# Attention and two feed-forward layers on one core: sign masks, score scale and diagonals placed anew

## The chip, the cores and the metric

The kernel runs on one core of a Trainium2 chip. The metric is device time in microseconds (us) of one execution, lower is better; the time of a kernel is the median of several runs. The five engines of the core run their own instruction queues in order: PE (TensorE: matrix products), DVE (VectorE), ACT (ScalarE), POOL (GpSimd) and SP (SyncE, which issues the DMA transfers).

## The reference, cut to what matters

```python
q, k, v: (4, 12, 448, 64)          # batch, heads, sequence, head size; float32
q_n, k_n = rmsnorm(q, g_q), rmsnorm(k, g_k)
attn = softmax(q_n @ k_n.T / sqrt(64))          # row maximum subtracted
x = (attn @ v) -> (1792, 768)
h = x @ w_in                       # (768, 2048)
x = (h * sigmoid(h)) @ w_out       # (2048, 768)
g = x @ w_gate                     # (768, 1536)
out = (silu(g) * (x @ w_val)) @ w_out2          # w_out2 (1536, 768)
```

The weights arrive as float64 and the result is float32.

## The kernel before, in words

Products are made in float16 pairs: a matrix is split in a high half and a low half (the rest), and three products of halves stand for one. The four batches are four blocks. A block has six pairs of heads. Block 0 is special: its first four pairs (`n < N0`) make their scores in float32 with one product, all others with float16 halves; and block 0's probabilities are turned by TensorE, those of the later blocks by DMA transposes. While block 0's attention runs, the chunks of `w_in` are prepared; while its first layer (`ffn1_h`, L1011) runs, those of `w_out`; the later blocks' attention overlaps with both layers of the block before (L1011 and `ffn1_o`, L1051); the gate, value and second output weights are prepared while the last block's layers run. From some 790 us on only the last layers run (L1206, L1250 to L1252).

*Scores* (`softmax_pair`): a score product (L701 in float32, L706 in float16) goes to PSUM, VectorE takes the negative row maximum (L715), a small operation scales it (L718 on ScalarE, L719 on VectorE, L720 on GpSimd), and ScalarE makes the exponential and its sum (L723), with a scale `eS`. In the later blocks high (L739 to L741) and low halves (L744 and L745 on GpSimd, L747 on VectorE) of the probabilities follow, a DMA transpose, and the product with V (L816).

*Weights* (`bring`, `convert`): a chunk of 128x768 float64 numbers lands in a staging tile as pairs of 32-bit words. A scaled copy of the high words, y, is made (L873 ACT, L874 DVE, L875 POOL). Then the sign must be put where it belongs, in one of two ways. With `sign` A or P the low word is shifted (L885) and ScalarE (L887) or GpSimd (L888) writes a float16 number with the sign into its upper half. With `sign` D VectorE masks the sign out of the high word (L879) and shifts some bits of the low word beside it (L880), and no other engine is needed. L890 merges, ScalarE squares and sums (L892), small operations make a scale (L450, L456, L457). Where the low half is made by TensorE (E in the tables, `pe_lo`), a diagonal of the scale is made first (`diag`, L905 on GpSimd, two buffers), the high half is written (L832 to L834), and two matrix products in two halves of 384 columns (L676 in float32, L677) give the low half, which ScalarE copies out (L679). In 14 chunks of `w_out` the low half is made so. Chunks 12 and 14 hold y in XT, chunks 13 and 15 in a raw tile of ATT, so the fourteenth waits for the twelfth.

After the last chunk the scales of all chunks are compared (L445, L971), a product (L441) and L442 spread the maximum, and G is multiplied by the result (L1041 to L1043) before the next layer's first product (L1051).

*The order.* Every operation is recorded with its possible engines, a cost in ns and a due time, and a planner (`Plan.emit`) plays the program through with these costs, giving each operation to an engine and each engine a fixed order. The tables in TUNE hold due times (`FINE`, `OFF`, `WIN`, `WOUT` and others), the allowed engines (letters A, D, P, E) and `WIS`, `WOS`, `GVS`, `O2S`, the sign's engine for each chunk of the five weight matrices. So a change of a cost or a due time moves instructions on every engine.

Of the kernel before, what the change touches and what calls it, by code (L numbers as in the profile page):

```python
# [21 lines left out]
    RIPE_SHORT=1505.0,
# [1 line left out]
    OFF={('load_v', 3): 422.1, ('pv', 3): 8.5, ('qk', 1): -85.8, ('load_qk', 0): -35.2, ('qk', 4): -10.1, ('v_scale', 1): -174.8, ('pv', 1): -9.5, ('soft', 0): -14.2, ('v', 0): -74.0, ('o', 1): 127.6, ('load_v', 0): 121.2, ('qk', 3): -4.5, ('load_v', 4): -203.1, ('h', 2): 116.5, ('v_scale', 2): 58.8, ('v_scale', 3): 122.8, 'w_out': 58.2, 'w_in': 30.8, ('qk', 0): 111.3, ('o', 0): 94.3, ('v', 1): 16.5, ('pv', 0): -6.2, ('h', 1): 362.6, ('v_scale', 0): 43.5, 'h0': -41.4, ('v', 3): 6.8, ('soft', 3): 8.0, ('v', 4): -72.8, 'gv': 130.5, 'x2': 181.6, ('load_qk', 3): 17.7, ('load_qk', 2): 93.7, 'o3': 150.3, 'w2': -104.8, ('v', 2): -25.3, ('load_qk', 4): -5.2, ('load_v', 1): -22.2, ('qk', 2): -34.1, 'f2': -90.5, ('pv', 2): 40.8, ('soft', 2): 61.8, ('pv', 4): 42.7, ('o', 2): 101.1, ('v_scale', 4): -228.9, ('load_v', 2): -52.2, ('load_qk', 1): 19.1, ('soft', 1): 11.3, ('h', 3): -109.0, ('soft', 4): 32.6},
# [6 lines left out]
    BI={'act': -64.7, 'dve': 190.7, 'pool': 150.6},
    T_ATT=109.3,
    STEP0=3.2,
    STEP=21.0,
    WIN=83.7,
    WOUT=99.3,
# [9 lines left out]
    GK=('D', 'P', 'DP'),
    QL=('D', 'D', 'P'),
    VH=('P', 'ADP', 'A'),
    VL=('DP', 'D', 'D'),
    XL=('D', 'D', 'D'),  # L50
# [14 lines left out]
    GVL=('DP', 'DP', 'DP', 'DP', 'DP', 'DP', 'DP', 'DP', 'DP', 'DP', 'D', 'DP', 'D', 'DP', 'DP', 'DP', 'DP', 'DP', 'DP', 'DP', 'P', 'DP', 'D', 'DP'),  # L65
    O2Y=('ADP', 'AP', 'AD', 'D', 'A', 'ADP', 'A', 'AD', 'AD', 'AD', 'AD', 'A'),
    O2S=('D', 'A', 'AP', 'P', 'D', 'D', 'D', 'D', 'D', 'D', 'D', 'P'),
    O2H=('A', 'A', 'DP', 'A', 'A', 'A', 'A', 'A', 'AD', 'A', 'AP', 'A'),
    O2L=('DP',) * 12,
    GH=('AP', 'AD', 'A', 'A'),  # L70
# [1317 lines left out]
```

## Time and profile before

| | |
|---|---|
| median of 3 runs | 1258.47 us (1258.27 to 1259.04) |
| the profiled execution, its own time | 1259.7 us |
| its span, first to last instruction | 1257.9 us |
| TensorE busy | 1178.2 us (94%) |
| VectorE, ScalarE, GpSimd busy | 687.2 us, 669.4 us, 492.0 us |
| mean granted TensorE clock | 0.98 of full speed |

Busy time is summed per engine; the wait of an engine is the idle time just ahead of an instruction, with the engine that ended it. A granted clock of 1 in a stretch means TensorE at 2.4 GHz all through; at the lower of its two levels it runs at 1.2 GHz. The matrix products are pipelined, so neighbouring rows of the timeline overlap by a little.

### The profile page before, as it was taken

The page shows a single profiled execution, that of the slowest core. Times are in us where ns is not written, and L with a number is a line of the kernel's source. Part 1 is how long each engine was busy: PE and PEld are TensorE (multiplying, and loading weights), DVE is VectorE, ACT ScalarE, POOL GpSimd, SP SyncE. Part 2 cuts the span into 40 slices and gives each one's busy share as a digit, 9 for nine tenths or more (in the row PEclk, how much of TensorE's full clock was granted, in tenths as well). Part 3 has the DMA queues.
Part 4 walks back from the last instruction along what each step waited for, and adds up shares of the span by engine and source line. Part 5 has one row for each costly group of instructions (what it writes and reads, how often), then busy time and mean ns, then how long its engine had stood idle before and what let it go on. Part 6 is the DMA issues. An engine that isn't in the chain of part 4 may idle for free.

```text
span 1257.9 us, 17505 instructions
## 1 busy us (share of the span) xinstructions
PE 1178.2 (94%) x6612; PEld 599.2 (48%) x6612; DVE 687.2 (55%) x1181; ACT 669.4 (53%) x1219; POOL 492.0 (39%) x474
## 2 busy tenths in 40 slices
PE   5989987799679999999999999999999999999998
PEld 3334443344334444444445454445544555446685
DVE  4788876688756575565459887873111301112121
ACT  4989967677669865898536435652111301112131
POOL 5565456454658897677721624120000100000000
PEclk9999999799889999999999999999999999999999
DMA  7565634479877688567774455502000101000101
GB/s 193 167 155 144 220 131 145 103 174 199 184 149 144 125 191 176 110 126 149 145 238 138 146 173 180 187 1 63 26 14 1 34 26 26 1 1 22 39 1 26
DMA packets 218581, 140.61 MB, mean 112 GB/s; under 512 B 156032, under 2 KB 210816, under 8 KB 218496
## 3 DMA queue, kind: packets, MB, share of 16 engines
q1 hardware_dynamic: 218496, 139.49, 44.3%
q8 instruction: 52, 0.85, 0.3%
q14 instruction: 33, 0.27, 0.1%
HBM read 85.79 MB, written 11.01 MB: 77 GB/s over the span
## 4 chain that ended last, share of the span: by engine, by line
PE 46%; DVE 5%; DMA 2%; POOL 1%; ACT 1%; issue 1%; POOLq 0%; ACTq 0%
PE ps L1206 25%; PE ps L1051 6%; PE ps L1250 4%; PE ps L1252 4%; PE ps L1251 4%; DMA ATT<-in_moe_w_val_dram 1%; DVE W L842 1%; PE ps L816 1%; PE ps L1011 1%; PE ps L706 1%; DVE ATT L890 1%; DVE G L1030 1%; DVE ATT L880 1%; DVE ATT L879 1%; DMA ATT<-ATT 1%
## 5 line engine op out<-in xcount | busy, mean ns | idle before, releaser
L1206 PE MATMUL ps<-XT,W 128*128 128x512 f16 (+1 forms) x1440 | 294.0, 352 | 3.8 <-ACT ER L1211 1.9
L1051 PE MATMUL ps<-G,W 128*128 128x448 f16 x1152 | 240.7, 355 | 4.0 <-DVE G L1041 4.0
L1011 PE MATMUL ps<-XT,W 128*128 128x448 f16 x1152 | 234.9, 353 | 8.2 <-ACT FT L1017 1.7
L1206 PEld LDWEIGHTS <-W 128*128 128x128 f16 x1440 | 141.0, 98 | 131.0 <-issue 5.1
L1011 PEld LDWEIGHTS <-W 128*128 128x128 f16 x1152 | 110.7, 99 | 120.5 <-issue 26.0
L1051 PEld LDWEIGHTS <-W 128*128 128x128 f16 x1152 | 107.9, 98 | 122.3 <-issue 28.9
L1216 ACT ACTIVATE G<-ER 128x512 f16<-128x512 f32 (+1 forms) x48 | 27.6, 575 | 167.3 <-DVE ER L1213 162.2
L1213 DVE SCALAR_TENSOR_TENSOR ER<-ER,ST,ps 128x512 f32<-128x512 f32 (+1 forms) x48 | 32.6, 680 | 151.5 <-PE ps L1206 151.4
L723 ACT ACTIVATE ER<-ps,ST 128x448 f32<-128x448 f32 x144 | 103.1, 719 | 12.1 <-POOL ATT L745 8.8
L1218 POOL TENSOR_SCALAR G<-ER 128x512 f16<-128x512 f32 x20 | 12.6, 629 | 245.5 <-DVE ER L1217 241.2
L715 DVE TENSOR_REDUCE ST<-ps 128x2 f32<-128x896 f32 x96 | 92.4, 966 | 27.8 <-PE ps L706 23.4
L1250 PE MATMUL ps<-W,G 128*128 128x384 f16 x308 | 100.4, 326 | 0.0
L1251 PE MATMUL ps<-W,G 128*128 128x384 f16 x308 | 100.4, 326 | 0.0
L1252 PE MATMUL ps<-W,G 128*128 128x384 f16 x308 | 100.4, 326 | 0.0
L1257 DVE SCALAR_TENSOR_TENSOR ATT<-ps,ST,ATT 128x384 f32<-128x384 f32 x28 | 17.3, 618 | 151.0 <-ACT ATT L1255 151.0
L1255 ACT ACTIVATE ATT<-ps,ST 128x384 f32<-128x384 f32 x28 | 16.2, 580 | 136.7 <-PE ps L1252 136.7
L745 POOL TENSOR_TENSOR ATT<-ER,ATT 128x448 f16<-128x448 f32 x77 | 86.0, 1117 | 6.4
L706 PE MATMUL ps<-ATT 128*64 128x448 f16 x560 | 75.3, 371 | 9.1 <-ACT ER L723 4.0
L1030 DVE SCALAR_TENSOR_TENSOR G<-FT,ST,G 128x448 f16<-128x448 f32 x64 | 57.5, 907 | 20.1 <-ACT G L1022 18.2
L744 POOL TENSOR_SCALAR ER<-ER,ST 128x448 f32<-128x448 f32 x77 | 56.7, 736 | 22.8 <-ACT ATT L739 11.8
L1206 PE MATMUL ps<-XT,ATT 128*128 128x512 f16 (+1 forms) x288 | 60.4, 352 | 0.0
L739 ACT ACTIVATE ATT<-ER,ST 128x448 f16<-128x448 f32 x71 | 45.5, 660 | 20.0 <-DVE ST L731 11.7
(221 smaller groups left out, 1889.4 us busy)
## 6 DMA issues: line engine op xcount, KB each, us to landing
ATT<-in_moe_w_out_dram SPq DMA_DIRECT2D x24, 768.0 KB, 4.3
W<-in_moe_w_in_dram SPq DMA_DIRECT2D x16, 768.0 KB, 6.1
ATT<-in_moe_w_gate_dram SPq DMA_DIRECT2D x12, 768.0 KB, 4.7
ATT<-in_moe_w_val_dram SPq DMA_DIRECT2D x12, 768.0 KB, 5.9
ATT<-in_q_dram SPq DMA_DIRECT2D x24, 224.0 KB, 3.1
ATT<-in_k_dram SPq DMA_DIRECT2D x24, 224.0 KB, 3.6
ATT<-in_v_dram SPq DMA_DIRECT2D x8, 672.0 KB, 7.2
x2d<-FT SPq DMA_DIRECT2D x24, 224.0 KB, 3.5
```

The costliest lines, as they stand in the source:

```text
L706: nc.tensor.matmul(out=sp[64 * h:64 * h + 64, u, 0:S], lhsT=T[:, 0, t, 64 * h:64 * h + 64], rhs=T[:, a, :, 64 * h:64 * h + 64], start=(a = ...
L715: op(DVE, 1.04 * S * nt + 65, lambda sp=sp, nm=nm, nt=nt: nc.vector.tensor_reduce(nm, sp[:, 0:nt, 0:S], AX.X, ALU.max, negate=True), r=sk, ...
L723: op(ACT, 705, lambda e=e, u=u, t=t, sp=sp: nc.scalar.activation(e, sp[:, u, 0:S], AF.Exp, bias=st["nb"][:, t:t + 1], scale=eS, accum_out= ...
L744: nc.gpsimd.tensor_scalar(e, e, r1, 1.0, ALU.mult, ALU.mult)
L745: nc.gpsimd.tensor_tensor(lo, e, hi, ALU.subtract)
L1011: nc.tensor.matmul(out=ps[:, 0:S], lhsT=w[:, a, kk], rhs=xt1((b * HP + kk) % NX, x), start=(kk == 0 and s == 0), stop=(kk == KD - 1 and s ...
L1030: DVE: (t_stt(S), lambda gt=gt, hi=hi, lo=lo, s1=s1: nc.vector.scalar_tensor_tensor(lo, gt, s1, hi, ALU.mult, ALU.subtract), True),
L1051: nc.tensor.matmul(out=ps[:, 0:S], lhsT=w[:, a, P * m:P * m + P], rhs=GV1[:, f, x], start=(f == 0 and s == 0), stop=(f == NF1 - 1 and s == 2))
L1206: nc.tensor.matmul(out=ps[:, 0:n], lhsT=w[:, aa, kk], rhs=xt2(kk, x)[:, 0:n], start=(kk == 0 and s == 0), stop=(kk == KD - 1 and s == 2))
L1250: nc.tensor.matmul(out=ps[:, 0, 0:384], lhsT=hi, rhs=wh, start=(f == 0), stop=(f == NF2 - 1))
L1251: nc.tensor.matmul(out=ps[:, 1, 0:384], lhsT=hi, rhs=wlo, start=(f == 0), stop=False)
L1252: nc.tensor.matmul(out=ps[:, 1, 0:384], lhsT=lo, rhs=wh, start=False, stop=(f == NF2 - 1))
```

## The change

1. For the first four pairs the factor of the keys is `g_q * g_k * 2^-25` and no longer scaled by the power of two that `eS` undoes, so the scores come out at their own scale: the row maximum is used as it is, the small operation (L718 to L720) is left out, and the exponential's scale is 1.
2. The planner's cost of a sign pass on ScalarE goes from about 793 to 1940 and on GpSimd from 880 to 2030, and in the tables the sign of 15 of the 16 chunks of `w_out` is D.
3. A diagonal may be made on VectorE as well.
4. The small scaling on VectorE is marked as one that shares with GpSimd, and the tables of due times and engines are other ones.

In all VectorE gets 11 sign pairs (L879, L880) more and 11 shifts (L885) fewer, GpSimd 9 sign passes and ScalarE 2 fewer; 13 of 15 diagonals are made on VectorE; 14 low halves of probabilities go from GpSimd to VectorE; 18 low halves of the last layers go from GpSimd to ScalarE. The number of TensorE's instructions is the same.

```diff
-    OFF={('load_v', 3): 422.1, ('pv', 3): 8.5, ('qk', 1): -85.8, ...
+    OFF={('load_v', 3): 411.6, ('pv', 3): 3.7, ('qk', 1): -77.7, ...
...
-    WOS=('P', 'P', 'P', 'AP', 'P', 'A', 'AP', 'AP', 'P', 'P', 'P', 'AP', 'AP', 'AP', 'P', 'D'),
+    WOS=('D', 'D', 'D', 'D', 'D', 'D', 'D', 'D', 'P', 'D', 'D', 'D', 'D', 'D', 'D', 'D'),
...
-    small(mult(gc, gc, g_s), ["gs"], ["gc"], 0)
+    small(lambda: nc.vector.tensor_scalar(gc, gc, 2.0 ** -25, None, ALU.mult), [], ["gc"], 0)
...
+            own = n < N0
+            top = nb if own else nm
...
-            add(only(TUNE["NB"][cl], {
...
+            if not own:
+                add(only(TUNE["NB"][cl], {
...
-                    e, sp[:, u, 0:S], AF.Exp, bias=st["nb"][:, t:t + 1], scale=eS, accum_out=st["sm"][:, t:t + 1]),
+                    e, sp[:, u, 0:S], AF.Exp, bias=st["nb"][:, t:t + 1], scale=1.0 if own else eS, accum_out=st["sm"][:, t:t + 1]),
...
-                ACT: (t_act(n) + 60, lambda: nc.scalar.activation(top, wide, AF.Copy, scale=2.0 ** -60)),
-                POOL: (880, lambda: nc.gpsimd.tensor_scalar(top, wide, 2.0 ** -60, 1.0, ALU.mult, ALU.mult))}), r=ykeys, w=skeys, due=need)
+                ACT: (1940, lambda: nc.scalar.activation(top, wide, AF.Copy, scale=2.0 ** -60)),
+                POOL: (2030, lambda: nc.gpsimd.tensor_scalar(top, wide, 2.0 ** -60, 1.0, ALU.mult, ALU.mult))}), r=ykeys, w=skeys, due=need)
...
-        op(POOL, 351, lambda: nc.gpsimd.tensor_scalar(dg, ID, s1, 2.0 ** 14, ALU.mult, ALU.mult), r=["id"] + sk, w=[("dgw", c)], due=due)
+        add({POOL: (351, lambda: nc.gpsimd.tensor_scalar(dg, ID, s1, 2.0 ** 14, ALU.mult, ALU.mult)),
+             DVE: (200, lambda: nc.vector.tensor_scalar(dg, ID, s1, 2.0 ** 14, ALU.mult, ALU.mult), True)}, r=["id"] + sk, w=[("dgw", c)], due=due)
```

How the order moves is shown at three places. The lines of the changed kernel are 3 higher from `softmax_pair` on (2 for L715, 4 from the diagonal on). The first is VectorE in the first pair's softmax, before:

```order
L715 TENSOR_REDUCE ST<-ps 128x2
L719 TENSOR_SCALAR ST<-ST 128x2
L633 TENSOR_REDUCE ST<-SQ 128x14
L715 TENSOR_REDUCE ST<-ps 128x2
L662 COPY ATT<-ps 64x4x64
L666 TENSOR_SCALAR ATT<-ps,ST 128x256
L666 TENSOR_SCALAR ATT<-ps,ST 128x192
L719 TENSOR_SCALAR ST<-ST 128x2
L715 TENSOR_REDUCE ST<-ps 128x2
```

and in the changed kernel:

```order
L717 TENSOR_REDUCE ST<-ps 128x2 x2
L633 TENSOR_REDUCE ST<-SQ 128x14
L666 TENSOR_SCALAR ATT<-ps,ST 128x256
L666 TENSOR_SCALAR ATT<-ps,ST 128x192
L717 TENSOR_REDUCE ST<-ps 128x2
```

The scalings behind the row maxima (L719) and the copy of transposed queries (L662, now on ScalarE) are gone. The second is VectorE at chunk 14 of `w_out`, the second that goes through XT, before:

```order
L874 TENSOR_SCALAR XT<-ATT 128x768
L874 TENSOR_SCALAR ATT<-ATT 128x768
L885 TENSOR_SCALAR ATT<-ATT 128x768
L879 TENSOR_SCALAR ATT<-ATT 128x768
L880 TENSOR_SCALAR ATT<-ATT 128x768
L1030 SCALAR_TENSOR_TENSOR G<-FT,ST,G 128x448
L890 SCALAR_TENSOR_TENSOR XT<-XT,ATT 128x768
L890 SCALAR_TENSOR_TENSOR ATT<-ATT 128x768
```

and in the changed kernel (L877 is the copy, L882 and L883 the sign pair, L893 the merge, L845 a low half):

```order
L893 SCALAR_TENSOR_TENSOR ATT<-ATT 128x768
L450 TENSOR_SCALAR ST<-ST 128x1
L877 TENSOR_SCALAR XT<-ATT 128x768
L456 TENSOR_SCALAR ST<-ST 128x1
L882 TENSOR_SCALAR ATT<-ATT 128x768
L457 RECIPROCAL ST<-ST 128x1
L883 TENSOR_SCALAR ATT<-ATT 128x768
L893 SCALAR_TENSOR_TENSOR XT<-XT,ATT 128x768
L845 SCALAR_TENSOR_TENSOR W<-ATT,ST,W 128x768
```

Chunk 15 is through before chunk 14 starts, and nothing of chunk 14 up to the merge is on another engine. The third is TensorE between chunks 12 and 14, the two that go through XT, before:

```order
L1011 LDWEIGHTS W
L1011 MATMUL ps<-XT,W 128x448
L676 MATMUL ps<-XT,DG 128x384
L677 LDWEIGHTS NI
L677 MATMUL ps<-W,NI 128x384
L676 MATMUL ps<-XT,DG 128x384
L677 LDWEIGHTS NI
L677 MATMUL ps<-W,NI 128x384
L452 MATMUL ps<-ST 128x1
```

and in the changed kernel:

```order
L677 LDWEIGHTS NI
L677 MATMUL ps<-W,NI 128x384
L676 MATMUL ps<-XT,DG 128x384
L677 LDWEIGHTS NI
L677 MATMUL ps<-W,NI 128x384
L676 MATMUL ps<-XT,DG 128x384
L677 LDWEIGHTS NI
L677 MATMUL ps<-W,NI 128x384
L441 MATMUL ps<-ID,ST 128x128
```

Before, six products of the first layer (L1011) stand between the two chunks; in the changed kernel chunk 14 follows chunk 12 directly, and the product that spreads the maximum (L441) stands ahead of the scores of block 1.

## Rows read from the trace of the kernel before

**Rows 1.** Windows: us; busy PE, PEld, DVE, ACT, POOL; PEclk; DMA share, GB/s.

```profile
138.20:197.70 59.50, 53.45 (x252) 27.17 (x250) 45.32 (x93) 46.97 (x76) 33.69 (x26) 0.97 0.48 168
197.70:220.90 23.20, 15.42 (x60) 7.47 (x60) 17.39 (x33) 16.00 (x29) 12.08 (x12) 0.91 0.47 129
220.90:232.90 12.00, 5.74 (x18) 2.94 (x19) 8.81 (x30) 8.28 (x16) 3.27 (x4) 0.64 0.15 35
318.00:360.00 42.00, 27.77 (x157) 12.45 (x156) 31.30 (x52) 24.91 (x51) 21.89 (x18) 0.80 0.94 196
400.00:800.00 400.00, 389.89 (x2226) 187.21 (x2225) 273.44 (x459) 258.42 (x474) 241.45 (x234) 1.00 0.65 160
800.00:1258.00 458.00, 452.62 (x2562) 250.45 (x2559) 117.08 (x181) 108.52 (x183) 26.05 (x34) 1.00 0.09 26
```

**Rows 2.** TensorE's waits from 120 to 235 us: in total, times, longest.

```profile
PE ps L676 <- POOL DG L905: 12.6, 4, 8.1
PE ps L1051 <- DVE G L1041: 4.0, 1, 4.0
```

**Rows 3.** Timeline of DVE, POOL, ACT, PE, last chunks: start, us; [idle before <- releaser].

```profile
197.67 0.67 DVE L874 TENSOR_SCALAR XT<-ATT 128x768 f32<-128x768 f32 x1
...
213.20 1.53 DVE L874 TENSOR_SCALAR XT<-ATT 128x768 f32<-128x768 f32 x1 [2.61 <-PE ps L676]
214.65 0.55 DVE L874 TENSOR_SCALAR ATT<-ATT 128x768 f32<-128x768 f32 x1
...
216.17 2.59 DVE L880 TENSOR_SCALAR ATT<-ATT 128x768 uint16<-128x768 uint16 x1
...
219.12 0.95 DVE L890 SCALAR_TENSOR_TENSOR XT<-XT,ATT 128x768 int32<-128x768 int32 x1
...
215.76 2.12 POOL L888 TENSOR_SCALAR ATT<-ATT 128x768 f16<-128x768 f32 x1 [1.45 <-DVE ATT L885]
221.78 0.73 POOL L905 TENSOR_SCALAR DG<-ID,ST 128x128 f32<-128x128 f32 x1 [3.90 <-DVE ST L457]
...
220.10 0.84 ACT L892 ACTIVATE ATT<-XT 128x768 f32<-128x768 f32 x1 [4.27 <-DVE XT L890]
...
220.95 2.43 ACT L517 ACTIVATE ATT<-ATT 128x2688 f32<-128x2688 f32 x1
...
211.47 0.88 PE L676 MATMUL ps<-XT,DG 128*128 128x384 f32 x2
...
213.16 1.30 PE L1011 MATMUL ps<-XT,W 128*128 128x448 f16 x6
222.56 1.65 PE L676 MATMUL ps<-XT,DG 128*128 128x384 f32 x2 [8.10 <-POOL DG L905]
...
232.93 1.27 PE L1051 MATMUL ps<-G,W 128*128 128x448 f16 x3 [4.04 <-DVE G L1041]
```

**Rows 4.** VectorE's groups from 138.2 to 197.7: busy us, mean ns | idle before <- releasers.

```profile
L890 DVE SCALAR_TENSOR_TENSOR W<-W 128x768 int32<-128x768 int32 x6 | 7.8, 1301 | 7.0 <-POOL W L888 4.5 <-ACT W L887 2.5
L890 DVE SCALAR_TENSOR_TENSOR W<-W,ATT 128x768 int32<-128x768 int32 x7 | 6.6, 948 | 2.6 <-POOL ATT L888 2.6
...
L842 DVE SCALAR_TENSOR_TENSOR W<-W,ST 128x768 f16<-128x768 f32 x4 | 4.3, 1090 | 0.3 <-ACT W L832 0.3
```

**Rows 5.** Timeline of VectorE and ScalarE at the first exponential.

```profile
19.52 1.18 DVE L719 TENSOR_SCALAR ST<-ST 128x2 f32<-128x2 f32 x1
...
20.79 0.72 ACT L723 ACTIVATE ER<-ps,ST 128x448 f32<-128x448 f32 x1 [1.83 <-DVE ST L719]
```

**Rows 6.** Durations: two lines (ns min/median/max) and one group of VectorE.

```profile
L879 DVE TENSOR_SCALAR ATT<-ATT x28: 547/558/2256, 215.6 to 811.3; 128x768 int32<-128x768 int32 x28
...
L880 DVE TENSOR_SCALAR ATT<-ATT x28: 1018/1033/2586, 216.2 to 812.4; 128x768 uint16<-128x768 uint16 x28
...
L490 DVE TENSOR_SCALAR GX<-GX,ST 128x64 f32<-128x64 f32 x1 | 0.3, 254 | 0.0
```

**Rows 7.** TensorE's waits from 318 to 360 us: in total, times, longest.

```profile
PE ps L816 <- DMA ATT<-ATT: 5.9, 2, 3.7
```

More of the change, by code (lines that the diff above doesn't have):

```diff
@@ L21 @@
     RIPE=0.0,
[L22 removed]
+    RIPE_SHORT=1543.0,
     PATIENCE={'silu': 2351.866, 'exp': 6600.368},
[L24 removed]
@@ L29 @@
+    WIY=('A', 'AP', 'DP', 'P', 'ADP', 'D', 'AP', 'AP', 'ADP', 'AP', 'AP', 'AP', 'DP', 'DP', 'ADP', 'AD'),
+    WOY=('D', 'D', 'D', 'DP', 'D', 'D', 'D', 'AP', 'D', 'AD', 'P', 'D', 'DP', 'D', 'D', 'D'),
+    CUT=(0, 1, 2, 6, 10, 13, 16),
+    SLACK=157.0,
     SLACK2=13.0,
     WT={'act': 0.85, 'dve': 0.99, 'pool': 0.5},
[L31 to L36, printed above, removed]
+    BI={'act': -220.7, 'dve': 190.7, 'pool': 227.0},
@@ L37 @@
+    T_ATT=109.9,
+    STEP0=3.4,
+    STEP=21.1,
+    WIN=93.5,
+    WOUT=92.8,
     ATT1=2.8,
-    PHI1=('AD',) * 7,
-    PHI2=('ADP',) * 7,
+    PHI1=('AD', 'AD', 'AD', 'A', 'A', 'AD', 'AD'),
+    PHI2=('ADP', 'ADP', 'ADP', 'AD', 'ADP', 'AD', 'ADP'),
     PTE=('D', 'A', 'A', 'A', 'A', 'AD', 'AD'),
@@ L42 @@
     PLO1=('DP', 'D', 'DP', 'DP', 'DP', 'DP', 'D'),
-    PLO2=('P', 'P', 'P', 'DP', 'P', 'P', 'P'),
-    RK=('DP', 'P', 'P'),
+    PLO2=('P', 'P', 'P', 'DP', 'P', 'DP', 'P'),
+    RK=('P', 'P', 'P'),
     RQ=('D', 'DP', 'DP'),
[L46 to L50, printed above, removed]
+    GK=('DP', 'P', 'DP'),
+    QL=('P', 'D', 'P'),
+    VH=('AD', 'ADP', 'A'),
+    VL=('D', 'D', 'D'),
+    XL=('E', 'D', 'D'),
     WARM=(12, 7, 6),
     N0=4,
-    TQ='AD',
+    TQ='A',
     TK='D',
@@ L65 @@
[L65 to L70, printed above, removed]
+    WOS=('D', 'D', 'D', 'D', 'D', 'D', 'D', 'D', 'P', 'D', 'D', 'D', 'D', 'D', 'D', 'D'),
@@ L71 @@
+    O2Y=('ADP', 'AP', 'AD', 'D', 'A', 'ADP', 'A', 'AD', 'AP', 'AD', 'ADP', 'A'),
+    O2S=('AP', 'D', 'D', 'P', 'D', 'P', 'D', 'A', 'D', 'A', 'D', 'A'),
+    O2H=('AP', 'A', 'AP', 'A', 'AP', 'AP', 'AP', 'AP', 'A', 'AP', 'AP', 'AP'),
+    O2L=('D', 'ADP', 'D', 'A', 'P', 'D', 'D', 'AP', 'D', 'A', 'D', 'D'),
+    GH=('ADP', 'DP', 'AP', 'A'),
     GL=('DP', 'D', 'D', 'DP'),
@@ L714, in softmax_pair @@
             sm, rr = st["sm"][:, t0:t0 + nt], st["rr"][:, t0:t0 + nt]
-            op(DVE, 1.04 * S * nt + 65, lambda sp=sp, nm=nm, nt=nt: nc.vector.tensor_reduce(nm, sp[:, 0:nt, 0:S], AX.X, ALU.max, negate=True),
-               r=sk, w=[("nm", i, g)], due=due)
-            add(only(TUNE["NB"][cl], {
-                ACT: (200, lambda nm=nm, nb=nb: nc.scalar.activation(nb, nm, AF.Copy, scale=eS)),
-                DVE: (130, lambda nm=nm, nb=nb: nc.vector.tensor_scalar(nb, nm, eS, None, ALU.mult)),
-                POOL: (246, lambda nm=nm, nb=nb: nc.gpsimd.tensor_scalar(nb, nm, eS, 1.0, ALU.mult, ALU.mult))}), r=[("nm", i, g), "eS"], w=[("nb", i, g)], due=due)
+            own = n < N0
+            top = nb if own else nm
+            op(DVE, 1.04 * S * nt + 65, lambda sp=sp, top=top, nt=nt: nc.vector.tensor_reduce(top, sp[:, 0:nt, 0:S], AX.X, ALU.max, negate=True),
+               r=sk, w=[("nb" if own else "nm", i, g)], due=due)
+            if not own:
+                add(only(TUNE["NB"][cl], {
+                    ACT: (200, lambda nm=nm, nb=nb: nc.scalar.activation(nb, nm, AF.Copy, scale=eS)),
+                    DVE: (130, lambda nm=nm, nb=nb: nc.vector.tensor_scalar(nb, nm, eS, None, ALU.mult), True),
+                    POOL: (246, lambda nm=nm, nb=nb: nc.gpsimd.tensor_scalar(nb, nm, eS, 1.0, ALU.mult, ALU.mult))}), r=[("nm", i, g), "eS"], w=[("nb", i, g)], due=due)
             for u, t in enumerate(tiles):
                 e, ek = es[t]
-                op(ACT, 705, lambda e=e, u=u, t=t, sp=sp: nc.scalar.activation(
-                    e, sp[:, u, 0:S], AF.Exp, bias=st["nb"][:, t:t + 1], scale=eS, accum_out=st["sm"][:, t:t + 1]),
+                op(ACT, 705, lambda e=e, u=u, t=t, sp=sp, own=own: nc.scalar.activation(
+                    e, sp[:, u, 0:S], AF.Exp, bias=st["nb"][:, t:t + 1], scale=1.0 if own else eS, accum_out=st["sm"][:, t:t + 1]),
                    r=[sk[u], ("nb", i, g)], w=ek + [("sm", i, t)], due=due, table="exp")
```

18 lines of the change are left out of this document (8 added, 10 removed).

## Prediction

> **What bounds the kernel now.** I read busy time and granted clock by stretch first. From 800 us on TensorE is busy 452.6 of 458 us, from 400 to 800 it is busy 389.9 of 400 [rows 1]: whatever the change does to the other engines there, it can return about 10 us at most. The time that can be won lies ahead of 400 us, where an engine that feeds TensorE is late. So I went to TensorE's own waits in the stretch where `w_out` is prepared: 12.6 us in four waits for a diagonal made on GpSimd, 8.1 of them in one, and 4.0 us for the first product of the next layer [rows 2]. The timeline of the last chunks shows the order of events [rows 3]: VectorE starts the first chunk that goes through XT at 197.67, its product runs on TensorE at 211.47, the second XT chunk may overwrite XT only then (213.20), its signs are on GpSimd until 217.9, its diagonal is written at 221.78, TensorE restarts at 222.56 and the next layer's first product starts at 232.93. In the 12 us before that the granted clock is 0.64, part of the stretch at the lower of the two levels (1.2 GHz) [rows 1], and the same product takes 1.65 us instead of 0.88 [rows 3]: TensorE had stood still for 8.1 us.
>
> What keeps the chunks is told by VectorE's groups from 138.2 (its first low half of G) to 197.7: it is busy 45.3 of 59.5 us [rows 1], and of its 14.2 idle us 7.1 (4.5 + 2.6) end with a sign pass on GpSimd [rows 4].
>
> **The change, part by part.** The profiled execution took 1259.7 us (span 1257.9), 1.2 us above the median 1258.47 of the runs shown. Sums are made against the profiled time.
>
> *Scores at their own scale (first four pairs).* The small scaling between the row maximum and the exponential goes. The first one took 1.18 us on VectorE because it stood beside GpSimd's work, and ScalarE sat idle 1.83 us until it was done [rows 5]. Sixteen such operations go, but ScalarE is busy nearly all of the time afterwards, so most of them are covered by other exponentials. Copies of the transposed queries move to ScalarE and cost a little of it back. Bounds 0 and -4 us (1 us in each of the four pairs); taken: **-2 us**, near that one idle time.
>
> *Signs on VectorE, diagonals on VectorE.* I take VectorE from its first low half of G to the first XT chunk. By the program order it issues there 12 more half-word shifts of 1.03 us (the median, [rows 6]) = 12.4; 12 more maskings of 0.56 [rows 6] less 10 word shifts of the same size = 1.1; 10 diagonals; two more low halves of G and some eight other operations, together 3.4. A diagonal of 128x128 float32 on VectorE is not in the trace: the nearest rows are 0.25 us for 128x64 and 0.56 for 128x768 [rows 6], and I take 0.3, near the smaller, so 3.0; at the ends 2.5 and 5.6. Sum +19.9 us of work. What goes: the 7.1 us of waiting for GpSimd's signs, and the stretching of the merges beside GpSimd, 1301 against 948 ns, six times, 2.1 us [rows 4]. Of the other 7.1 us of idle I let 3.5 go, since a queue that holds more work of its own finds the other engines' results ready. The first XT chunk starts 19.9 - 7.1 - 2.1 - 3.5 = **7.2 us later** in the stage.
>
> From there to the next layer the path gets shorter. For the second XT chunk the scaled copy took 1.53, the sign pass on GpSimd 2.12 and the bit shift of its neighbour 2.59 us; from 213.20 to the end of the merge (219.12 + 0.95) 6.9 us went by [rows 3]. The order of the change runs copy, mask, shift and merge on one engine: 0.55 + 0.56 + 1.03 + 0.95 = 3.1, **-3.8 us**. The first XT chunk waited for a sign pass on ScalarE and for a diagonal behind other work of GpSimd: 197.67 to 211.47 is 13.8 us [rows 3]. In the new order VectorE does 4.4 us up to the merge (copy, a neighbour's merge, masking, diagonal and shift, its own merge), ScalarE squares (0.84, [rows 3], and some 0.2 for reading the sum), and VectorE does 2.5 us up to the diagonal (a low half of 1.09, [rows 4], a copy, a masking, the diagonal): 7.9, **-5.9 us**. ScalarE's square over v (2.43 us at 220.95) now stands behind the last weight square instead of ahead of one; I count nothing for it, since the reduction that follows on VectorE waits for it. What takes the cover away: in the new order of TensorE nothing of the first layer is left between the two XT chunks, so it waits out the whole preparation of the second, some 5 us, in place of 1.3 us of work and 8.1 of waiting. The stage's end moves by 7.2 - 3.8 - 5.9 = **-2.5 us**; with the rest of that idle gone as well it is -6.1, with no more gone than GpSimd's 7.1 it is +1.0.
>
> *Block 1.* TensorE waits 5.9 us for two transposes of probabilities (3.7 and 2.2 us) ahead of the fifth and sixth product with V [rows 7], between 318 and 360 us, where VectorE is busy 31.3, ScalarE 24.9 and GpSimd 21.9 of 42 us [rows 1]: no engine is full, the pair's chain is. In the new order sixteen score products stand directly behind the fourth product with V, and directly behind the fifth; before, 21 and 9 products of the layers stood ahead of them, at some 0.2 us each (six took 1.30, [rows 3]) 4.2 and 1.8 us. GpSimd also has fewer low halves to make (14 over the kernel go to VectorE). Bounds 0 and -5.9; taken **-3 us**, since the two leads are 6.0 together and the softmax of a pair still needs three engines.
>
> *The rest.* The gate and value weights get three masks fewer on VectorE and more high halves on ScalarE, both beside TensorE's work, which is 97% busy there [rows 1]: 0, and at most a few microseconds either way if a chunk comes late. Low halves in the last layer move from GpSimd to ScalarE, while TensorE runs without a gap: 0.
>
> Sum: -2 - 2.5 - 3 = -7.5; 1259.7 - 7.5 = 1252.2, and as a median (1.2 lower) **1251 us**.
>
> **The rivals.** *VectorE becomes the bound of the `w_out` stage, and the kernel gets slower.* The stage gives VectorE 19.9 us more work, and in the order printed every step of a chunk but the square now queues on it. If its idle time stays as it is (14.2 us) the first XT chunk starts 17.8 us later, not 7.2, and the stage ends 8.1 us later. The row for it is a shift that took 2.59 us while GpSimd's sign pass ran from 215.76 to 217.88 [rows 3]: it ended 0.9 us after that pass, so it was held. The Trainium skill, SBUF — State Buffer, section Who interferes with whom, says that VectorE and GpSimd share a port pair as an exclusive lock, and that an operation with one input outside the two-port modes does not contend; by the lock every mask that meets GpSimd waits, by the exception the shift would not have, and this row sides with the lock. Priced from the row, each mask that meets GpSimd costs 1.56 us; two or three of 12 would, since GpSimd has 13 operations in that stretch of its order, where it had 38: 4 us. Then -2 + 8.1 + 4 = +10, and with or without block 1's 3 us 1266 to 1269. It decides from the point where the first XT chunk starts more than 9.7 us later in the stage (what the tail gives back), about 11.7 with the start's 2 us. For it: 45.3 + 19.9 is more than 59.5. Against it: half the idle time there is waiting for just the passes that go.
>
> *The diagonals were the whole story.* All 12.6 us of waits for diagonals go, and VectorE's idle time with them; half of the 4.0 ahead of the next layer goes too, since the last scales come sooner; with -2 and -3 elsewhere and some microseconds for the gap between the XT chunks left: about -16, 1242. For it: GpSimd loses 9 sign passes and 13 diagonals in this stage. Against: the same chunks must pass VectorE.
>
> *Nothing arrives.* VectorE's added work eats the stage's gain (+1.0), the start gains 2, and block 1 nothing, because a transpose that starts sooner meets the next pair's loads (the DMA engines are 0.94 busy there, [rows 1]): 1259.7 - 1 - 1.2 = 1257.5. That the change does not do what it says is covered here: if the scheduler left signs on GpSimd, but the printed order has 11 sign pairs more on VectorE in all and 9 passes fewer on GpSimd.
>
> **How the numbers follow.** Forecast (1247 to 1255): 0.42. Diagonals the whole story (1238 to 1247): 0.23. Nothing arrives (1256 to 1261): 0.16. VectorE the bound (1261 to 1269): 0.19. A measurement of this kernel can tell about 0.2%, 2.5 us, from no change; so faster 0.65, same 0.16, slower 0.19. The range 1239 to 1268 leaves out the outer ends of the second and last case, under 0.1.
>
> **What would show it.** Right: TensorE's waits for a diagonal fall from 12.6 us to under 8, the first product of the next layer starts some 4 us sooner (near 228 to 229), its waits for a transposed probability fall to about 3 us, and the idle time from 400 on stays near 10 + 5 us. Wrong: VectorE is busy over nine tenths from 140 to 220 and the second XT chunk's copy starts after 216 (the first rival), masks of over 2 us appear beside GpSimd (its price), or new waits of TensorE show up between 650 and 800 for weights that come late.

## The result and the profile after

The changed kernel takes **1238.18 us** (median of 4 runs, 1235.70 to 1240.69) beside 1258.76 for the kernel before (4 runs): ratio 0.9837, 95% interval 0.9816 to 0.9858, or 20.6 us less. The forecast was 7.5 less, with a range of 1239 to 1268. In two later comparisons the ratio was 0.9815 [0.9792, 0.9839] and 0.9821 [0.9796, 0.9846].

The profiled execution took 1238.76 us, its span 1236.9 (before 1257.9): 21.0 less. TensorE's busy time fell from 1178.2 to 1172.6 for the same number of products: fewer stretches ran at the lower of the two clock levels (mean granted clock 0.985 for 0.98). The other 15.4 us are idle time of TensorE. Working out idle as length less busy, by stretch: 0 to 140 us, 25.6 before and 20.6 after; 140 to 240, 20.1 and 13.0; 240 to 400, 18.5 and 19.2; 400 to 800, 10.1 and 6.2; from 800 on, 5.3 and 5.3.

Four windows of the changed kernel answer to [rows 1] (us; busy PE, PEld, DVE, ACT, POOL; PEclk; DMA share, GB/s): the stage from VectorE's first low half of G to the first XT chunk, its end, block 1's softmax, and 400 to 800 us.

```profile
130.40:192.40 62.00, 58.58 (x280) 29.56 (x278) 59.89 (x124) 50.23 (x89) 12.59 (x10) 1.00 0.49 177
...
206.50:216.90 10.40, 5.67 (x19) 2.86 (x20) 7.37 (x24) 9.33 (x14) 3.10 (x3) 0.67 0.14 44
300.00:342.00 42.00, 26.72 (x168) 13.74 (x165) 27.70 (x52) 24.32 (x52) 23.66 (x18) 0.84 1.02 204
400.00:800.00 400.00, 393.82 (x2238) 190.12 (x2235) 272.75 (x479) 272.94 (x488) 203.05 (x188) 1.00 0.63 162
```

VectorE is now busy 59.9 of 62 us in that stage (before 45.3 of 59.5), GpSimd 12.6 (before 33.7). TensorE's waits from 120 to 235 us, as in [rows 2]:

```profile
PE ps L676 <- POOL DG L908: 6.1, 1, 6.1
PE ps L676 <- ACT W L679: 2.7, 3, 1.4
PE ps L1055 <- DVE G L1045: 2.2, 1, 2.2
```

The timeline of the last chunks, as in [rows 3] (L877 copy, L882 and L883 sign pair, L893 merge, L908 diagonal on GpSimd, L1055 the next layer; VectorE, GpSimd, then TensorE):

```profile
192.42 0.56 DVE L877 TENSOR_SCALAR XT<-ATT 128x768 f32<-128x768 f32 x1
192.90 0.95 DVE L893 SCALAR_TENSOR_TENSOR ATT<-ATT 128x768 int32<-128x768 int32 x1
193.76 0.56 DVE L882 TENSOR_SCALAR ATT<-ATT 128x768 int32<-128x768 int32 x1
...
203.34 0.56 DVE L877 TENSOR_SCALAR XT<-ATT 128x768 f32<-128x768 f32 x1
...
204.53 1.03 DVE L883 TENSOR_SCALAR ATT<-ATT 128x768 uint16<-128x768 uint16 x1
...
205.59 0.96 DVE L893 SCALAR_TENSOR_TENSOR XT<-XT,ATT 128x768 int32<-128x768 int32 x1
...
208.26 0.72 POOL L908 TENSOR_SCALAR DG<-ID,ST 128x128 f32<-128x128 f32 x1 [10.42 <-DVE ST L445]
...
201.02 0.91 PE L676 MATMUL ps<-XT,DG 128*128 128x384 f32 x2 [0.85 <-ACT W L679]
...
209.04 1.65 PE L676 MATMUL ps<-XT,DG 128*128 128x384 f32 x2 [6.13 <-POOL DG L908]
...
216.87 1.47 PE L1055 MATMUL ps<-G,W 128*128 128x448 f16 x4 [2.19 <-DVE G L1045]
```

The next layer's first product starts at 216.87 in place of 232.93: 16.1 of the 21.0 us are won by there, and the same 946 products stand ahead of it in both kernels.

### The profile page after: what moved, and what is told of

Read it like the earlier page. It is cut to its first block, busy times and chain, and to the rows that moved or that the text cites. A ratio compares the mean times of both kernels' runs of the same rounds, so it can differ in the third digit from the quotient of the medians.

```text
span 1236.9 us, 17468 instructions
## 1 busy us (share of the span) xinstructions
PE 1172.6 (95%) x6612; PEld 600.4 (49%) x6612; DVE 678.7 (55%) x1210; ACT 693.5 (56%) x1260; POOL 402.6 (33%) x374
## 4 chain that ended last, share of the span: by engine, by line
PE 47%; DVE 3%; DMA 1%; ACT 1%; issue 1%; POOL 1%; ACTq 0%; POOLq 0%; DVEq 0%
PE ps L1210 25%; PE ps L1055 7%; PE ps L1254 4%; PE ps L1256 4%; PE ps L1255 4%; DVE W L845 1%; DVE G L1034 1%; DVE ATT L893 1%; PE ps L819 1%; PE ps L1015 1%; DMA ATT<-in_moe_w_out_dram 0%; DMA x2d<-FT 0%; DVE ATT L883 0%; PE ps L706 0%; DMA ATT<-in_moe_w_val_dram 0%
## 5 line engine op out<-in xcount | busy, mean ns | idle before, releaser
L1055 PE MATMUL ps<-G,W 128*128 128x448 f16 x1152 | 241.4, 355 | 2.2 <-DVE G L1045 2.2
L1055 PEld LDWEIGHTS <-W 128*128 128x128 f16 x1152 | 108.1, 98 | 120.4 <-issue 26.7
L1015 PEld LDWEIGHTS <-W 128*128 128x128 f16 x1152 | 110.9, 99 | 114.5 <-issue 19.3
L726 ACT ACTIVATE ER<-ps,ST 128x448 f32<-128x448 f32 x144 | 102.3, 713 | 14.6 <-POOL ATT L748 7.5
L717 DVE TENSOR_REDUCE ST<-ps 128x2 f32<-128x896 f32 x96 | 92.1, 966 | 31.8 <-PE ps L706 25.7
L706 PE MATMUL ps<-ATT 128*64 128x448 f16 x560 | 74.1, 362 | 5.5 <-ACT ER L726 3.0
L748 POOL TENSOR_TENSOR ATT<-ER,ATT 128x448 f16<-128x448 f32 x63 | 71.7, 1138 | 5.3
L742 ACT ACTIVATE ATT<-ER,ST 128x448 f16<-128x448 f32 x84 | 53.2, 659 | 10.8 <-DVE ST L734 6.5
L819 PE MATMUL ps<-ATT 128*64 128x448 f16 x396 | 44.6, 377 | 14.3 <-DMA ATT<-ATT 14.2
```

The source lines that it names most:

```text
L706: nc.tensor.matmul(out=sp[64 * h:64 * h + 64, u, 0:S], lhsT=T[:, 0, t, 64 * h:64 * h + 64], rhs=T[:, a, :, 64 * h:64 * h + 64], start=(a = ...
L717: op(DVE, 1.04 * S * nt + 65, lambda sp=sp, top=top, nt=nt: nc.vector.tensor_reduce(top, sp[:, 0:nt, 0:S], AX.X, ALU.max, negate=True), r= ...
L726: op(ACT, 705, lambda e=e, u=u, t=t, sp=sp, own=own: nc.scalar.activation(e, sp[:, u, 0:S], AF.Exp, bias=st["nb"][:, t:t + 1], scale=1.0 i ...
L748: nc.gpsimd.tensor_tensor(lo, e, hi, ALU.subtract)
L819: nc.tensor.matmul(out=PS_X[64 * h:64 * h + 64, 0:S], lhsT=vv[:, h, b, :], rhs=PT[:, :, b, 64 * h:64 * h + 64], start=(s == 0), stop=(s == ...
L1015: nc.tensor.matmul(out=ps[:, 0:S], lhsT=w[:, a, kk], rhs=xt1((b * HP + kk) % NX, x), start=(kk == 0 and s == 0), stop=(kk == KD - 1 and s ...
```

## The experiments

Most kernels below keep **every queue in the order that the planner gave it**: an edit is made where an operation is emitted, not where it is planned, so TensorE's and SyncE's queues are the same row for row, and only the operation in question changes its engine or goes (the order of the changed kernel is the new order, that of the kernel before the old one). That separates the edits from the new order, which the diff alone mixes. Events of the profiled executions (us; "product 1" is the first of the first layer, "product 2" the first of the next, XT the copies of the two chunks through XT):

| kernel | product 1 | XT, XT | product 2 | span | from product 2 to the end |
|---|---|---|---|---|---|
| before | 120.4 | 197.7, 213.2 | 232.9 | 1257.9 | 1025.0 |
| g1: own scale | 114.3 | 192.7, 208.3 | 228.0 | 1252.5 | 1024.5 |
| g2: signs | 121.1 | 195.1, 209.9 | 228.5 | 1251.0 | 1022.5 |
| g3: diagonals | 120.4 | 196.0, 211.0 | 230.8 | 1253.4 | 1022.6 |
| g4: all three | 114.9 | 188.7, 203.6 | 222.7 | 1246.1 | 1023.5 |
| changed kernel | 112.4 | 192.4, 203.3 | 216.9 | 1236.9 | 1020.0 |
| f1: scaling back | 116.2 | 197.3, 208.2 | 221.5 | 1240.2 | 1018.7 |
| f2: diagonals back | 112.5 | 191.9, 203.6 | 217.2 | 1233.6 | 1016.4 |
| f3: signs back | 110.9 | 197.9, 211.6 | 226.1 | 1243.3 | 1017.2 |
| f5: all back | 118.8 | 205.4, 219.8 | 234.1 | 1252.0 | 1018.0 |
| r1: old tables | 111.7 | 199.2, 215.7 | 231.1 | 1251.8 | 1020.7 |

Three profiles of the changed kernel itself differ by 1.3 us in product 2 and 1.9 in the span; less than that between two rows says nothing.

### The edits in the old order (g1 to g4)

```diff
-            op(DVE, ..., nm=nm, nt=nt: nc.vector.tensor_reduce(nm, ...
+            op(DVE, ..., top=nb if n < N0 else nm, nt=nt: nc.vector.tensor_reduce(top, ...
-                DVE: (130, lambda nm=nm, nb=nb: nc.vector.tensor_scalar(nb, nm, eS, ...
+                DVE: (130, lambda nm=nm, nb=nb, own=n < N0: None if own else nc.vector.tensor_scalar(nb, nm, eS, ...
...
-            op(DVE, 470, lambda: nc.vector.tensor_scalar(lw, lw, 29, ...
+            op(DVE, 470, mask if mine else lambda: nc.vector.tensor_scalar(lw, lw, 29, ...
-                POOL: (880, lambda: nc.gpsimd.tensor_scalar(top, wide, ...
+                POOL: (880, slip if mine else lambda: nc.gpsimd.tensor_scalar(top, wide, ...
...
-        op(POOL, 351, lambda: nc.gpsimd.tensor_scalar(dg, ID, ...
+        op(POOL, 351, lambda: nc.vector.tensor_scalar(dg, ID, ...
```

The first part is g1, the second g2 (mask and slip are the two operations of L879 and L880, for `w_out` alone), the third g3; g4 has all.

> The kernel before with every queue in its old order; only the scores of the first four pairs come at their own scale, and the small scalings there (L718 to L720) are left out. Theory A (the edit itself is worth what the first four pairs gained, since the exponential waited for a scaling that stood behind other work in VectorE's queue): the first product of the first layer moves from 120.4 to about 113, the kernel to about 1251 (-8 us). Theory B (the edit is worth the -2 us that I gave it; the rest of the 8 us came from the new order): 1255 to 1258.

Measured: 0.9961 [0.9946, 0.9976], 4.9 us: between the two theories. Product 1 comes 6.1 us sooner by this edit alone, three quarters of the 8.0 that the whole change gains there. What the 6.1 us consist of is read below, in the part on the prediction: 2.2 are waiting, 3.9 a faster TensorE.

> The kernel before with every queue in its old order; only the sign pass of 15 chunks of w_out (GpSimd or ScalarE) is replaced, in its place, by the mask and the half-word shift on VectorE. Theory A (the passes between the engines are what the stage loses): the second XT chunk's preparation shortens by some 3 to 4 us, VectorE's 7.1 us of waiting for signs go, the next layer's first product comes 4 to 6 us sooner than 232.9, the kernel ends near 1253. Theory B (VectorE's queue is full in that order, and the masks only pay in the new one): within 2 us of before, or up to 5 us slower.

Measured: 0.9949 [0.9931, 0.9966], 6.4 us; product 2 is 4.4 us sooner. Theory A. VectorE has 54.6 us of work from 140 to 200, where it had 45.8, and still the first XT chunk starts 2.6 us earlier: its waits for GpSimd's signs (7.1 us) are gone.

> The kernel before with every queue in its old order; only the diagonals are made on VectorE, in their place, instead of GpSimd. Theory A (diagonals were late because they stood behind GpSimd's sign passes): TensorE's 12.6 us of waits for diagonals fall under 5, the next layer's first product comes 6 to 8 us sooner, the kernel ends near 1251. Theory B (the diagonal was late because its scale was): the same waits stay, now for VectorE, at 8 us or more, and the time stays within 2 us of before.

Measured: 0.9967 [0.9955, 0.9980], 4.2 us, between the two theories. The wait behind the second XT chunk stays, now for VectorE; the small ones go:

```profile
PE ps L676 <- DVE DG L905: 9.9, 2, 8.6
```

> The kernel before with every queue in its old order and all three edits at once: scores at their own scale, signs of w_out on VectorE, diagonals on VectorE. If the edits make the gain: near 1240, at most 3 us above the changed kernel's 1238.2. If the new order of the queues makes most of it: above 1248. Rival of the prediction (VectorE becomes the bound): above 1255, with VectorE busy over nine tenths from 140 to 220 us.

Measured: 0.9917 [0.9896, 0.9938], 10.4 us: half of the gain, and less than the 15.5 us that the three edits gave one by one. The order of the old tables holds the rest. In it VectorE copies the second XT chunk at 203.57 and merges it only at 209.06, since chunk 15 goes through the same queue between the two; the diagonal still waits:

```profile
PE ps L676 <- DVE DG L905: 8.5, 3, 7.7
PE ps L1051 <- DVE G L1041: 3.8, 1, 3.8
```

### The edits undone in the new order (f1, f2, f3, f5, f6)

f1 puts a multiplication by 1 behind each row maximum of the first four pairs; f2 and f6 emit the 13 diagonals with `nc.gpsimd`; f3 puts the word shift and the sign pass in the place of the mask and the half-word shift; f5 does all.

> The changed kernel with every queue in its order; only a scaling (by 1) is put back on VectorE directly behind each row maximum of the first four pairs. In the kernel before, taking the scalings out of the old order gave 5 us; there they stood up to three operations behind their maximum. Theory A (what they cost was their place in the queue): directly behind the maximum each costs its own 0.2 to 0.6 us on a VectorE that is 0.75 busy, so the first product of the first layer moves by 1 to 3 us and the kernel ends 1 to 3 us later, 1239 to 1241. Theory B (the hop itself is what costs): some 6 us later, near 1244.

Measured: 0.9875 [0.9839, 0.9911], 5 to 8 us above the changed kernel by the ratios, 3.3 by the spans; product 1 is 3.9 us later. Between the two theories, and more than A: the sixteen operations are 5.7 us of VectorE (12 of 0.42, 4 of 0.15), and product 1 feels 3.9 of that, though nothing stands between the maximum and its scaling. In the old order (g1) it was 6.1; the 2.2 us between are little more than the 1.1 by which product 1 differs between profiles of the changed kernel.

> The changed kernel with every queue in its order; the 13 diagonals made on VectorE are made on GpSimd, in their place. GpSimd is busy only 10 of the 60 us from 140 to 200 in that order. Theory A (a diagonal was late because GpSimd was full): it now costs only its longer duration and the way to another engine, 0 to 3 us, 1238 to 1241. Theory B (VectorE is the right place whatever the load): 6 us or more, above 1244.

> The changed kernel with every queue in its order and the 13 diagonals on GpSimd, as in f2_diagonals_back, now beside the changed kernel. There the next layer's first product came at 217.19, in the changed kernel at 216.87. If diagonals on VectorE are worth nothing in the new order: within 2 us of the changed kernel. If they are a loss there: 3 to 5 us faster than it, as the two separate comparisons with before (0.9797 and 0.9837) have it. If they are a gain: 2 us or more slower.

Measured: 0.9797 [0.9757, 0.9837] in f2, 0.9814 [0.9787, 0.9840] in f6, beside 0.9815 for the changed kernel on the same chip. Nothing: what looked like a gain in f2 was scatter. With one sign pass of `w_out` left on GpSimd, a diagonal is as good there; TensorE then waits 2.9 us for diagonals that it did not wait for, and 1.8 less for ScalarE.

> The changed kernel with every queue in its order; the signs of 14 chunks of w_out are put on GpSimd (one on ScalarE) again, in their place, with the word shift on VectorE. Theory A (the new order leans on signs being on VectorE; a chunk now waits for a pass of about 2 us in the middle of VectorE's queue): each of the chunks that follow each other closely adds 1 to 2 us, the next layer's first product comes 10 to 20 us later than 216.9, the kernel ends between 1248 and 1260. Theory B (the signs' engine matters little and the order makes the gain): within 6 us, the same size as in the old order, 1238 to 1245.

Measured: 0.9885 [0.9851, 0.9920]: 6 to 9 us above the changed kernel by the ratios, at the upper end of theory B. Product 2 comes 9.2 us later, just short of theory A's 10 to 20, twice what the signs were worth in the old order, but the span only 6.4; the difference lies behind product 2, within what the last column scatters. It is not quite a way back: f3 makes 14 signs of `w_out` on GpSimd and one on ScalarE, the kernel before made 10 and 5.

> The changed kernel with every queue in its order and all three edits undone in their place: the scaling behind the maximum, diagonals and signs on GpSimd. The old order with the three edits gave 0.9917 of before, half of the gain. If the two halves simply add (edits 10 us, order 10 us): near 1249. If the new order only works with the edits: at the old time of 1258 or slower, up to 1270.

Measured: 0.9940 [0.9919, 0.9960], nearer to a sum of two halves than to no gain. The new order alone gives about 7 us, and by the table none of it ahead of product 2 (234.1, before 232.9): the first XT chunk comes 7.7 us later and the way from it to product 2 is 6.6 us shorter (28.7 for 35.3). There the order pays only with the edits. What it gives is behind: from product 2 to the end the kernels that keep the new order take 1015 to 1020 us, those that keep the old one 1022 to 1025. No run takes that part of the order apart.

### What makes the order, and what holds the stage's end

> The code of the changed kernel (own scale, the new costs of a sign pass, diagonals on either engine), planned anew with the tables of the kernel before, except that w_out's signs are on VectorE as in the change. Theory A (the planner makes a good order by itself once the costs are right): near the changed kernel, 1238 to 1243. Theory B (the new due times and engines in the tables make the order): what the three edits gave in the old order, 1248 to 1252, or worse.

Measured: 0.9943 [0.9922, 0.9964], theory B. The planner, with the corrected costs and free diagonals but the old due times and engines, reaches product 1 as soon as the changed kernel and then loses all of it in the stage. Its waits for diagonals add up to more than in any other kernel:

```profile
PE ps L676 <- POOL DG L908: 19.5, 5, 7.7
```

All diagonals of `w_out` are on GpSimd there, but GpSimd was not what was late. The first stands at 177.6 us (166.3 in the changed kernel), and in this row of GpSimd's own waits it waits for the scale from VectorE, which is busy 48.6 of 60 us from 140 to 200, in the changed kernel 58.0:

```profile
POOL DG L908 <- DVE ST L457: 30.1, 4, 25.6
```

The tables hold due times and allowed engines; which of the two leaves VectorE idle there no run separates.

The next two move chunk 14 out of XT; the planner orders anew.

```diff
-                y, yk = XT[:, 12 * S:12 * S + 1536].bitcast(F32), [...]
+                y, yk = (ER[:, 2:4]..., [("e", 2), ("e", 3)]) if c == 14 else (XT[...].bitcast(F32), [...])
```

> The changed kernel with chunk 14 of w_out in a part of ER in place of XT, so that it need not wait until TensorE has read chunk 12; the planner then orders anew around it. TensorE's longest wait in the changed kernel (6.1 us, for chunk 14's diagonal) lies there. Theory A (sharing XT holds the end of the stage): that wait falls under 3 us, the next layer's first product comes 3 to 5 us sooner than 216.9, the kernel ends near 1234. Theory B (VectorE, 0.96 busy from 140 to 200, holds it; the shared tile costs nothing): the product comes within 2 us of 216.9 and the kernel within 3 us of 1238.

Measured: 0.9820 [0.9794, 0.9847]. Product 2 at 214.57, 2.3 us sooner, TensorE's longest wait 4.1 in place of 6.1, and no gain in the kernel: TensorE is idle 22.1 us from 300 to 400, 4 more than in the changed kernel. So the shared tile holds at most some 2 us of the end (the planner's order moved too), and block 1 took them back.

> As x1_third_tile, but chunk 14 lies in the first raw tile of ATT, where the next block's first q and k are loaded afterwards. Theory A: as there, less what the later load costs: 1234 to 1238. Theory B: within 3 us of 1238, or slower where the load delays block 1.

Measured: 0.9985 [0.9973, 0.9998]: product 2 at 222.46, and idle 29.4 us from 300 to 400 (100 less 70.65 busy). The planner's new order here is worse in both places; on the shared tile it says nothing.

> The changed kernel with every queue in its order; the two diagonals still made on GpSimd are made on VectorE. The last one took 0.72 us there and starts 0.17 us after its scale; VectorE has a high half of 0.62 us and a small operation ahead of it. Gain of the next layer's first product by 0 to 1 us; the kernel within 2 us of the changed one, 1236 to 1240.

Measured: 0.9792 [0.9774, 0.9810]. The wait for the last diagonal falls from 6.13 to 5.65, as the rows foretold. By the ratios the kernel is 3 to 6 us faster than the changed one; its interval overlaps those of the two later comparisons, but not the first. y1, below, has the same diagonals and stands beside the changed kernel on one chip.

### Block 1's transposes

In block 1 TensorE's waits for transposed probabilities rose (below). SyncE's queue, where each transpose of probabilities stands for 3.6 to 5.0 us, has its rows nearly end to end from 280 to 340. h1 and h2 take three loads per pair out of it.

```diff
-        op(SP, ..., lambda: nc.sync.dma_start(out=dst[0:64], in_=src), ...
+        op(SP, ..., lambda: (nc.gpsimd if b == 1 else nc.sync).dma_start(out=dst[0:64], in_=src), ...
```

> The changed kernel with every queue in its order; only the three loads of v of each pair of block 1 (0.65 us of SyncE's queue each, 1.9 of some 17 us per pair) are issued by GpSimd. In the changed kernel TensorE waits 13.1 us for transposed probabilities between 290 and 345, and SyncE's queue has no gap from 280 to 340. Theory A (SyncE's queue, where every transpose takes 3.6 to 5 us, sets the pace of block 1): a pair passes some 2 us sooner, the waits for transposes fall from 13 to under 8, the kernel gains 2 to 5 us. Theory B (the DMA engines, busy 1.03 in that stretch, set the pace): the waits stay at 11 to 15 us and the time within 2 us of the changed kernel.

> As h1_v_on_gpsimd, but the loads of v of block 1 are issued from ScalarE's queue. Theory A: SyncE's queue is relieved as much, but ScalarE, 0.76 busy in block 1, takes the issues into its own queue, between the exponentials: waits for transposes under 10 us, waits for exponentials up by 1 to 3, the time 0 to 4 us below the changed kernel. Theory B: waits for transposes stay, the time is the same or up to 3 us above.

Measured: 0.9829 [0.9804, 0.9853] and 0.9809 [0.9785, 0.9834], beside 0.9815 for the changed kernel. Theory A falls: TensorE still waits for the transposed probabilities ahead of the same two products, 8.9 us in h1 and 11.5 in h2, part of it now put down to the softmax that feeds them; in h1:

```profile
PE ps L819 <- DMA ATT<-ATT: 6.9, 1, 6.9
PE ps L706 <- ACT ER L726: 4.6, 5, 2.0
PE ps L441 <- DVE ST L1065: 2.6, 1, 2.6
PE ps L819 <- DVE ST L734: 2.0, 1, 2.0
```

> The changed kernel with every queue in its order, all diagonals on VectorE (as in f4_last_diagonals, where the next layer's first product came at 215.70) and the loads of v of block 1 issued from ScalarE's queue (as in h2_v_on_scalar). Alone each was at most 0.3% below the changed kernel, inside what the intervals allow. If both are real: 3 to 5 us below the changed kernel beside it. If they were scatter: within 2 us of it.

Measured: 0.9809 [0.9783, 0.9835], the changed kernel beside it 0.9821: the same within the noise. No version was found that is measurably faster than the changed kernel.

## Why the prediction was wrong, step by step

**The start: -2 forecast, -7.8 found** (VectorE's first low half of G at 130.44 for 138.19; product 1 8.0 sooner). The step that failed is pricing the sixteen operations by "that one idle time" alone: the sum has waits and no term for TensorE's clock, which it puts at nothing without a reason. Four windows from 0 to product 1, in the kernel before, g1, f1 and the changed kernel, columns as in [rows 1]:

```profile
0.00:120.37 120.37, 96.02 (x528) 47.56 (x529) 89.32 (x159) 95.09 (x189) 69.52 (x75) 0.94 0.61 168
0.00:114.30 114.30, 92.13 (x528) 47.05 (x529) 82.65 (x149) 92.32 (x189) 67.52 (x69) 0.97 0.63 172
0.00:116.24 116.24, 94.52 (x526) 48.34 (x527) 84.95 (x163) 92.71 (x189) 65.84 (x65) 0.96 0.62 170
0.00:112.39 112.39, 92.20 (x526) 47.32 (x527) 80.69 (x147) 92.38 (x189) 65.07 (x65) 0.97 0.64 176
```

In g1 the same 528 products take 92.1 us of TensorE's busy time in place of 96.0, at a granted clock of 0.97 for 0.94, and its idle time (length less busy) falls from 24.4 to 22.2. So 3.9 of the 6.1 us are faster products and 2.2 are waiting, the forecast's -2. g2 and g3, which keep the scaling, have 97.1 and 95.8 us busy there; g4, which leaves it out, has 93.1. In the whole change 3.8 of the 8.0 us are busy time and 4.2 waiting, just past my lower bound of -4, so the new order adds 2.0 of waiting; the operations put back (f1) cost 2.3 and 1.5. The waiting went down although ScalarE was not "busy nearly all of the time": 113.5 of the first 140 us before, so 26.5 were open (11.3 of them waits for the first loads), and the chain of a pair (scores in one of two PSUM buffers, maximum, scaling, exponential, next scores in that buffer) passed through every scaling.

**The stage up to the first XT chunk: 7.2 us longer forecast, 2.5 found** (59.5 to 62.0). Two terms were off. The added work was put at 19.9 less 2.1 of stretching, 17.8; VectorE's busy time rose by 14.6. I had added durations of rows, and rows of VectorE overlap: the copy at 192.42 lasts 0.56 and the next operation starts 0.48 later. The 124 rows of the stage add up to 71.2 us for 59.9 of busy time, the 93 of before to 51.9 for 45.3: 19.3 us more of durations, near the forecast, but only 14.6 more of busy time. And the idle time, of which I let 10.6 go, fell by 12.1, from 14.2 to 2.1, nearly all: with most signs on VectorE there is always something to do. g2 shows the same in the old order. TensorE was nearly full in this stage as well, busy 58.6 of 62 us with 28 more products in it than before (53.5 of 59.5), so a longer stage is not a loss: its own idle time there fell from 6.0 to 3.4.

**From there to the next layer: -9.7 forecast, -10.8 found** (35.3 to 24.5). Right, and by its own parts: the second XT chunk from its copy to the end of its merge 3.2 us (6.9 before; -3.7 for -3.8 forecast), the first from its copy to its product 8.6 (13.8; -5.2 for -5.9). The last 1.9 us are the end of the merge to product 2, less 0.6 between the two. The wait of TensorE between the two chunks is 6.1, forecast at some 5. But g4 has the same edits and keeps 34.0 us there, and f5 has the new order without them and needs 28.7: most of this gain comes from the order, where chunk 15 stands ahead of chunk 14, as the second excerpt of the orders showed.

**Block 1: -3 forecast, nothing found.** The waits for transposes were to fall from 5.9 to 3 us; they rose to 12.1 at the same two products ([rows 7]; TensorE's timeline, L819 is the product with V):

```profile
315.01 4.32 PE L819 MATMUL ps<-ATT 128*64 128x448 f16 x22 [5.08 <-DMA ATT<-ATT]
...
333.19 3.92 PE L819 MATMUL ps<-ATT 128*64 128x448 f16 x22 [7.03 <-DMA ATT<-ATT]
```

The products with V of the second to sixth pair stand 17.6 us apart on average before (278.70 to 349.00) and 16.7 after (266.58 to 333.19): a pair's chain takes nearly as long. I had read score products that "stand directly behind the fourth product with V" as a lead of 6 us; but with the layers' products taken from between, TensorE only comes to the wait sooner. These two products start 17.0 and 15.8 us earlier than before, about the 16.1 that were won by product 2. The idle time from 300 to 400 is 17.7 before and 18.1 after. What sets the pace of 16 to 18 us is not SyncE's queue alone (h1, h2); whether it is the softmax's chain or the DMA engines, busy 1.00 of the time from 280 to 340, stays open.

**The rest: 0 forecast, about -4 found.** Idle from 400 to 800 fell from 10.1 to 6.2, within the few microseconds that I allowed and in one direction. It goes with the order, not with the edits (the last column of the table).

In sum: -5.8 (start), -4.7 (stage), -1.1 (tail), and -2.0 behind product 2 (-5.0 found, -3 forecast) make, before rounding, the 13.5 us by which -7.5 missed -21.0. Of these, 5.6 are TensorE's busy time (3.8 ahead of product 1, 1.7 behind product 2), for which the forecast had no term. Of the signs named beforehand, the waits for a diagonal (6.1, under 8) and the idle time from 400 on (11.5 for 10 + 5) came as said; product 2 came 16 us sooner in place of 4, and the waits for transposes rose.

**The rivals.** "The diagonals were the whole story" has the nearest time (1242) for the wrong reason: diagonals gave 4.2 us in the old order (g3) and nothing in the new (f6), and the largest wait for one is still there. "VectorE becomes the bound" named its first sign rightly (busy 0.92 from 140 to 220) but not its second (the second XT copy after 216; it came at 203.3): VectorE was full, with less work than I had added up, and no mask took over 1.9 us. "Nothing arrives" fails by the 20.6 us; only its part on block 1 came true. The price of the second rival exists, but few operations paid it: of the twelve half-word shifts in the stage eleven took 1.0 us, and one took 1.61:

```profile
186.02 1.61 DVE L883 TENSOR_SCALAR ATT<-ATT 128x768 uint16<-128x768 uint16 x1
...
185.81 0.93 POOL L837 TENSOR_SCALAR W<-W,ST 128x768 f16<-128x768 f32 x1 [1.85 <-PE ps L1015]
```

GpSimd's operation began 0.21 us ahead of the shift and ended at 186.74; from there to the shift's end at 187.63 it is 0.89 us, nearly a whole shift. In the kernel before, all five such shifts that began while a GpSimd operation ran ended 0.87 to 0.89 us after it. The Trainium skill, SBUF — State Buffer, section Who interferes with whom, has an exclusive lock for this pair, held for a whole instruction, and exempts VectorE's operations with one input outside the two-port modes. The rows agree with the lock. No run shows in which mode the shift ran, so neither these rows nor the prediction's speak against the exemption. GpSimd had 10 operations in the stage (26 before), so few shifts met one.

## What to carry to other kernels

Where a change takes waits away from TensorE, price its clock too: here leaving out sixteen operations won 2.2 us of waiting and 3.9 of faster products, and only busy and idle time read apart show it. Add up an engine's start-to-start times, not its durations. And where a change brings new tables of due times, try the edits in the old order and the old operations in the new one: here the order alone gave some 7 us, the edits alone some 10 and both 21, and the forecast had costed the edits only.

## What the runs showed of the hardware

A sign pass (768 float32 to float16 written at every fourth place) took 1.89 to 2.49 us on GpSimd in the 13 that f3 puts back there (1.90 where no VectorE row stood beside it) and 1.91 to 2.03 on ScalarE in the kernel before, about twice the 0.9 of their contiguous passes over as many numbers. In the changed kernel one on GpSimd beside a shift and a merge of VectorE took 2.60, and the merge 2.27 for 0.95. A diagonal of 128x128 float32 took 0.28 on VectorE (estimated at 0.3); on GpSimd the last one took 0.72, and in r1 the fifteen took 0.37 to 1.76. Issuing a load of v took about 0.6 us on ScalarE's and on GpSimd's queue (h2, h1), as on SyncE's.
